# Pacing a weave by VectorE work and moving one block's queries and softmax one dense layer ahead, in a two-layer linear-attention kernel

## The chip, the cores and the metric

The kernel runs on one core of a Trainium2 chip. The metric is device time in microseconds (us) of one execution; the time before is the median of 3 runs. Engines are named as the profile names them: PE (TensorE, matrix multiplications and transposes), PEld (its weight loads), DVE (VectorE), ACT (ScalarE), POOL (GpSimd) and SP (SyncE, which here issues nearly all transfers). Each engine works through its own queue in order, so an instruction that waits holds up all that stand behind it on that engine.

## The reference

Two layers, each an attention block A and a dense block B, with the same weights in both layers. There are 2048 rows of D = 576, 32 heads of 18, and a hidden width F = 4608.

```
x = A_x
x = x + A(layernorm(x));  x = x + B(layernorm(x))      # layer 0
x = x + A(layernorm(x));  x = x + B(layernorm(x))      # layer 1

A(x): q, k, v = x @ wqkv, split into 32 heads of 18
      pq, pk = q @ w_phi, k @ w_phi                    # per head, 18x18
      phi(p) = concat(softmax(p), softmax(-p))         # 36 features
      kv = sum over rows of phi(pk)^T v;  z = sum over rows of phi(pk)
      o  = (phi(pq) @ kv) / (phi(pq) . z + 1e-6)
      return o @ wo
B(x): r = relu(x @ w1 + b1);  return (r*r) @ w2 + b2
```

## The kernel before

**Tiling.** The 2048 rows are four blocks of 512, each four tiles of 128 rows. A product in float32 accuracy is made of three products of rounded parts: each operand is split into a high part (an ACT copy to the type fp32r) and a low part (the operand less its high part, on DVE or POOL). Every such split therefore is an ACT instruction with a DVE or POOL instruction behind it. Names that end in `h` and `l` are these two parts.

**Dense layer** (`g_mlp`). For one block it walks over 36 slices f of the hidden width. A step loads the slice's weights (`m_0r` in the trace), splits them into `m_0h` (of w1) and `m_0s` (of w2), makes the hidden values `m_0ph` in 14 matmuls, squares and splits them into `m_0hb`, and adds the slice before to the output `m_0acc` in 15 matmuls. On DVE a step is three subtractions: `m_0h` (L696), `m_0s` (L697, a part of it on POOL at L698) and `m_0hb` (L718). Each step ends with a `yield`.

**Attention of a block** (`g_attend`), also a generator of small steps: `g_q` makes the four query tiles on PE (`a_3q`, `a_3qp`), `g_soft` the two softmaxes of a tile (DVE, POOL, ACT; tiles `Q0` to `Q3`), `g_phi` the normaliser (two steps a tile, tiles `m` and `u`), `g_out` transposes the features and multiplies them by kv (eleven steps, tiles `pt`, `fh`, `fl`, `pn`, `oh`, `ol`), and the norm steps multiply by wo (`po`), add the residual and normalise, so that the next dense layer can begin. `g_out` has two PSUM buffers in these stages: one holds `pt`, the other the open sum `pn`.

**The weave.** `weave(main, other, rate)` runs a dense layer and takes `rate` steps of the next blocks' attention per dense step, each step counting 1 whatever it holds. Behind the weave stands a scheduler that gives each engine its order: an instruction may be moved ahead of others on its engine where the scheduler thinks that the engine would stand idle. `tc.issue_after` limits this: what is written under it stays behind a named instruction of the same engine. `held` puts a generator's steps behind the latest `m_..hb`.

**Layer 1**, which is all that the change touches. The stages are, in order: a barrier that finishes the attention of block 1 (names `t1`); the dense layer of block 1 (`m_1`), woven with the attention of block 0 (`a_0`) at rate 1.0; the dense layer of block 0 (`m_0`), woven with the attention of blocks 3 and 2 (`a_3`, `a_2`) at rate 2.2; and last `g_pair`, the dense layer of blocks 3 and 2 taken together with seven products of half size in place of eight. `g_norm_first` and `g_norm_second` prepare the pair's operands: the second one forms sums and differences of the two blocks' halves in `combine` (names `a_2nu`, `a_2nt1` and so on, many small operations on DVE, POOL and ACT). The pair's own weights go through `load_pair` and `split_pair` (names `m_3r`, `m_3w`, `m_3s`). Before its loop the pair does this for its first two slices:

```
        drain(split_pair(0, load_pair(0)))
        raw = load_pair(1)
        for k in range(NP):
```

`split_pair(0)` borrows one of the two buffers `h1` and one of the two buffers `r1`, through which the dense layer before moves its own weights `m_0h` and `m_0r`.

Of the kernel before, what the change touches and what calls it, by code (L numbers as in the profile page):

```python
# [7 lines left out]
F32 = mybir.dt.float32  # L8
# [5 lines left out]
P = 128  # L14
TB = 512
# [6 lines left out]
def layers_kernel(  # L22
# [19 lines left out]
    S, D = x_in.shape[1], x_in.shape[2]  # L42
# [9 lines left out]
    NC = KC + 1  # L52
# [9 lines left out]
    TP = 3 * TW  # L62
# [32 lines left out]
    def drain(gen):  # L95
        for _ in gen:
            pass

    def weave(main, other, rate):

        due = 0.0
        for _ in main:
            due += rate
            while due >= 1.0 and next(other, other) is not other:
                due -= 1.0
        drain(other)

    def lagged(n, produce, consume, by=1):

# [63 lines left out]
    def new_slot(t, name, dtype=F32):  # L173
        return cst.tile([P, NC * P], dtype, name=name, tag=f"vslot{t}")
# [378 lines left out]
    def held(gen):  # L553

        while True:
            with tc.issue_after(dense["last"].ins):
                done = next(gen, gen) is gen
            if done:
                return
            yield  # L560

    def g_soft(raws, er, name, apart=0):
        for t in range(NT):
# [23 lines left out]
            ph.append(e)  # L587
            yield

    def g_out(layer, b, ph, dst, name, parts=1, pause=None, behind=None, norm=None):  # L590

# [51 lines left out]
        for part in range(parts):  # L643
            for _ in lagged(2 * NG, lambda i: turn(part, i), lambda i, f: times(part, i, f), parts):
                if pause and part < parts - 1:
                    next(pause, None)
                yield
        yield
        pair = pair or pieces()

        def x_after(t):
# [17 lines left out]
            nc.gpsimd.tensor_add(x, x, b2t)  # L669
            nc.sync.dma_start(xm[b][t], x)  # L670

        yield from (norm or g_norm)(x_after, dst, f"{name}n", keep)


    def g_mlp(layer, b, x, after, name, behind=None):
# [165 lines left out]
    def g_norm_second(x_of, dst, name, then):  # L841
# [4 lines left out]
            return t[:, : HK * TB].rearrange("p (c n) -> p c n", c=HK)  # L846

        def prepare():
            for a, k in enumerate(("b11", "b21")):
                cols = slice(a * HK * TB, (a + 1) * HK * TB)  # L850
                hi, lo = (sb.tile([P, 2 * D], F32, tag="E", name=f"{name}{k}{p}", bufs=4)[:, : HK * TB] for p in "hl")
                nc.sync.dma_start(hi, pth[:, cols])
                nc.sync.dma_start(lo, ptl[:, cols])
                full.append(new_slot(a, f"{name}f{a}")[:TP, :TB])
                nc.sync.dma_start(full[a], ptt[:, a * TB : (a + 1) * TB])
                ops[k] = [two(hi.bitcast(F32R)), two(lo.bitcast(F32R))]

# [57 lines left out]
    def g_pair(layer, blocks, x, after, name):  # L915

        R = D - P
        accs, wide, high, wops = {}, {}, {}, {}
        accs[0] = [ps_a.tile([P, TB], F32, tag=f"acc{c}", name=f"{name}acc{c}") for c in range(NC)]

        def load_pair(k):
            tags = ((cst, "zb"), (sb, "xd")) if k % 2 == 0 else ((cst, "kbh"), (cst, "kbl"))
            cols = slice(2 * k * P, 2 * (k + 1) * P)
            raw = []
            for a, (pool, tag) in enumerate(tags):
                r = pool.tile([P, (HK + 1) * 2 * P], F32, tag=tag, name=f"{name}r{a}_{k}", bufs=1)
# [139 lines left out]

        drain(split_pair(0, load_pair(0)))
        raw = load_pair(1)
        for k in range(NP):
            f0, f1 = 2 * k, 2 * k + 1  # L1070
            prep = split_pair(k + 1, raw) if k + 1 < NP else iter(())
# [55 lines left out]
            return x  # L1127
        return get

    def g_attend(layer, b, x, raws, dst, name, behind=None, norm=None):  # L1130

        if raws is None:
            raws = []
            if x is None:
                x = unspill(b, f"{name}u")
            yield from g_q(x, wpair("q", name), raws, name)
        er, ph = [], []
        yield from held(g_soft(raws, er, name))
        yield from held(g_phi(layer, er, ph, name, True))
        yield from g_out(layer, b, ph, dst, name, behind=behind and behind["last"], norm=norm)  # L1140

    def barrier(layer, b, prev, x, xprev, kes, vpair):

# [60 lines left out]
    for layer in range(2):  # L1204
        ready, raws = barrier(layer, b, prev, x, xprev, kes, vpair)
        spare["tags"] = []
        nxt_raws = raws
        prev_rows = None
        for i, b in enumerate(order):
            n = f"{layer}_{b}"  # L1210
            if layer and i == 2:
                drain(g_pair(layer, order[2:], operands, rows, f"m{n}"))
                break
            nxt = {}
            keep = {}
            operands = {}

            def g_back(i=i, prev_rows=prev_rows, keep=keep, nxt=nxt, nxt_raws=nxt_raws, operands=operands):
                if prev_rows is not None:
                    pb, rows = prev_rows  # L1220
                    m = f"1_{pb}"
                    xk = {}
                    yield from g_norm(lambda t: rows[t], xk, f"n{m}")
                    if i < NB - 1:
                        spill(pb, xk)
                        vts = []
                        yield from g_v(xk, wpair("v", f"w{m}"), vts, f"v{m}")
                        es = []
                        yield from g_k(xk, wpair("k", f"w{m}"), es, f"k{m}",
                                       then=lambda t: kv_tile(1, vts[t], es[t], f"kv{m}_{t}"))  # L1230
# [50 lines left out]
```

## Time and profile before

| | |
|---|---|
| median of 3 runs | 2591.77 us (2591.14 to 2592.89) |
| the profiled execution | 2591.81 us |
| its span, first to last instruction | 2590.1 us |
| mean granted clock of PE | 0.988 |
| busy share: PE, PEld, DVE, ACT, POOL | 97%, 85%, 59%, 49%, 31% |
| layer 1: start of `m_1`, of `m_0`, of the pair | about 1521, 1782 and 2137 us |

The page gives the busy share of each engine over the span and in 40 slices; asked for stretches, the trace gives each engine's busy time in them with the granted clock of PE, that is the share of its full speed at which PE was let run. A stretch loses time in two ways: PE stands idle, or it works at a lower clock. The list of waits says which instruction stood waiting and for what; the list in order of time gives each instruction's start and duration, with the idle time before it in square brackets.

### The profile page before, as it was taken

How to read it: one execution, taken by the hardware profiler on the slowest of the kernel's cores; microseconds unless marked ns; L12 is line 12 of the kernel's file. 1: busy time of each engine (PE TensorE's matmuls, PEld its weight loads, DVE VectorE, ACT ScalarE, POOL GpSimd, SP SyncE). 2: the span in 40 equal slices, each digit the busy share in tenths (PEclk: the TensorE clock that was granted, in tenths of full speed). 3: DMA queues.
4: the chain of work that ended last, by engine and by line, in shares of the span. 5: the costliest groups of instructions: out<-in, count | busy, mean ns of one | idle time of the engine just before them, and what ended most of it. 6: DMA issues, size and time to landing. Idle time of an engine off the chain costs nothing.

```text
span 2590.1 us, 41423 instructions
## 1 busy us (share of the span) xinstructions
PE 2519.7 (97%) x15282; PEld 2211.0 (85%) x15282; DVE 1533.6 (59%) x2408; ACT 1266.7 (49%) x2177; POOL 797.6 (31%) x869
## 2 busy tenths in 40 slices
PE   8999999999999999999999999999899988999999
PEld 8998888888888888888889988889788776888888
DVE  7778844446755458466334987344856656544444
ACT  4344554445554445545544445534445445666543
POOL 3444311113222123123111523121322257555222
PEclk9998999999999999999999999999999998999999
DMA  7103333354334443343332234235334324333364
GB/s 249 57 22 95 99 114 93 112 178 126 97 87 140 142 126 101 88 153 97 101 97 85 57 94 129 83 105 180 92 95 160 97 92 138 110 101 109 102 200 153
DMA packets 276758, 295.03 MB, mean 114 GB/s; under 512 B 28906, under 2 KB 206826, under 8 KB 274250
## 3 DMA queue, kind: packets, MB, share of 16 engines
q1 hardware_dynamic: 275296, 289.68, 37.1%
q8 instruction: 119, 1.95, 0.3%
q10 hardware_dynamic: 1258, 2.70, 0.3%
q14 instruction: 85, 0.70, 0.1%
HBM read 249.39 MB, written 42.89 MB: 113 GB/s over the span
## 4 chain that ended last, share of the span: by engine, by line
PE 50%; DVE 7%; POOL 2%; issue 1%; ACT 1%; DMA 0%; DVEq 0%; POOLq 0%; SPq 0%; ACTq 0%
PE m_1ph L708 8%; PE m_1acc L735 6%; PE m_0ph L708 5%; PE m_3px L988 4%; PE m_0acc L735 4%; PE m_3acc L1017 3%; PE m_3acacc L1017 2%; PE m_3py L988 2%; PE m_1acc L726 2%; PE m_0acc L726 1%; PE m_3acacc L1007 1%; PE m_3pz L988 1%; PE m_3acc L1007 1%; PE m_3ach L1017 1%; PE t1opo L662 1%
## 5 line engine op out<-in xcount | busy, mean ns | idle before, releaser
L708 PE MATMUL m_0ph<-a_0nh,m_0h 128*128 128x512 f32 (+1 forms) x760 | 199.7, 389 | 8.0 <-DVE m_0h L696 7.9
L735 PE MATMUL m_0acc<-m_0s,m_0hb 128*128 128x448 f32 x864 | 201.7, 368 | 1.5 <-DVE m_0hb L718 1.5
L735 PE MATMUL m_1acc<-m_1s,m_1hb 128*128 128x448 f32 x864 | 199.3, 366 | 1.4 <-DVE m_1hb L718 1.4
L735 PEld LDWEIGHTS m_0acc<-m_0s,m_0hb 128*128 128x128 f32 x864 | 162.8, 189 | 24.0 <-DVE m_0hb L718 2.8
L735 PEld LDWEIGHTS m_1acc<-m_1s,m_1hb 128*128 128x128 f32 x864 | 161.8, 188 | 23.1 <-DVE m_1hb L718 2.3
L698 POOL TENSOR_TENSOR m_0s<-m_0r,m_0s 128x128 fp32r<-128x128 f32 x72 | 58.0, 806 | 361.2 <-ACT m_0s L694 331.2
L708 PEld LDWEIGHTS m_0ph<-a_0nh,m_0h 128*128 128x128 f32 x760 | 137.9, 191 | 36.4 <-DVE m_0h L696 9.9
L698 POOL TENSOR_TENSOR m_1s<-m_1r,m_1s 128x128 fp32r<-128x128 f32 x72 | 59.3, 824 | 322.1 <-ACT m_1s L694 312.6
L696 DVE TENSOR_TENSOR m_1h<-m_1r,m_1h 128x640 fp32r<-128x640 f32 x72 | 64.9, 902 | 155.4 <-ACT m_1h L693 155.4
L696 DVE TENSOR_TENSOR m_0h<-m_0r,m_0h 128x640 fp32r<-128x640 f32 x72 | 66.6, 926 | 122.0 <-ACT m_0h L693 119.4
L715 ACT ACTIVATE m_0hr<-m_0ph,b1t 128x512 f32<-128x512 f32 x72 | 49.4, 686 | 180.5 <-PE m_0ph L708 180.5
L715 ACT ACTIVATE m_1hr<-m_1ph,b1t 128x512 f32<-128x512 f32 x72 | 49.5, 687 | 171.5 <-PE m_1ph L708 171.5
L977 DVE TENSOR_TENSOR m_3s<-m_3r,m_3s 128x448 fp32r<-128x448 f32 x72 | 49.5, 688 | 95.3 <-ACT m_3s L976 93.5
L735 PE MATMUL m_2acc<-m_2s,m_2hb 128*128 128x448 f32 x432 | 99.7, 366 | 1.3 <-DVE m_2hb L718 1.3
L735 PE MATMUL m_3acc<-m_3s,m_3hb 128*128 128x448 f32 x432 | 99.6, 366 | 0.9 <-DVE m_3hb L718 0.9
L978 POOL TENSOR_TENSOR m_3s<-m_3r,m_3s 128x128 fp32r<-128x128 f32 x72 | 58.0, 805 | 134.5 <-ACT m_3s L976 127.9
L708 PE MATMUL m_2ph<-a_2nh,m_2h 128*128 128x512 f32 (+1 forms) x380 | 97.3, 384 | 0.3 <-DVE m_2h L696 0.3
L708 PE MATMUL m_3ph<-t0onh,m_3h 128*128 128x512 f32 (+1 forms) x380 | 95.7, 382 | 0.1
L708 PE MATMUL m_1ph<-t1onh,m_1h 128*128 128x512 f32 (+1 forms) x380 | 95.7, 382 | 0.0
L708 PE MATMUL m_1ph<-a_1nh,m_1h 128*128 128x512 f32 (+1 forms) x380 | 95.3, 381 | 0.0
L1017 PE MATMUL m_3acc<-m_3s,m_3hb 128*128 128x448 f32 x432 | 94.4, 366 | 0.1
L735 PEld LDWEIGHTS m_2acc<-m_2s,m_2hb 128*128 128x128 f32 x432 | 80.8, 188 | 12.3 <-DVE m_2hb L718 2.2
(2103 smaller groups left out, 7096.9 us busy)
## 6 DMA issues: line engine op xcount, KB each, us to landing
m_3r<-in_B_w SPq DMA_DIRECT2D x108, 288.0 KB
m_0r<-in_B_w SPq DMA_DIRECT2D x72, 288.0 KB
m_1r<-in_B_w SPq DMA_DIRECT2D x72, 288.0 KB
m_3r<-in_B_w SPq DMA_DIRECT2D x72, 256.0 KB
m_0r<-in_B_w SPq DMA_DIRECT2D x72, 256.0 KB
m_1r<-in_B_w SPq DMA_DIRECT2D x72, 256.0 KB
m_2r<-in_B_w SPq DMA_DIRECT2D x36, 288.0 KB
m_2r<-in_B_w SPq DMA_DIRECT2D x36, 256.0 KB
```

What stands on the lines that cost most here:

```text
L662: nc.tensor.matmul(pt[:, :HP], a, m[:w, g], start=(g == 0 and k == 0), stop=(g == NG - 1 and k == 2))
L696: nc.vector.tensor_sub(l1, r1, h1.bitcast(F32))
L698: nc.gpsimd.tensor_sub(s2[:, D + R : 2 * D], r2[:, R:], s2[:, R:D].bitcast(F32))
L708: nc.tensor.matmul(ph[:, cols], a, m, start=(k == 0), stop=(k == len(ops) - 1))
L715: nc.scalar.activation(hr, ph, AF.Relu, bias=b1t[:, f : f + 1])
L726: nc.tensor.matmul(acc[KC], a, m, start=(f == 0 and k == 0), stop=(f == NF - 1 and k == 2))
L735: nc.tensor.matmul(acc[t][:, :R], a[:, rows], m, start=(f == 0 and k == 0), stop=(f == NF - 1 and k == 2))
L977: nc.vector.tensor_sub(s2[:, D : D + R], r2[:, :R], s2[:, :R].bitcast(F32))
L978: nc.gpsimd.tensor_sub(s2[:, D + R : 2 * D], r2[:, R:], s2[:, R:D].bitcast(F32))
L988: nc.tensor.matmul(ps, a, m, start=start and i == 0, stop=i == len(ms) - 1, skip_group_check=True)
L1007: nc.tensor.matmul(accs[b][KC], a, m, start=(g == 0 and k == 0), stop=(g == NF - 1 and k == 2))
L1017: nc.tensor.matmul(accs[b][t][:, :R], a[:, rows], m, start=(g == 0 and k == 0), stop=(g == NF - 1 and k == 2))
```

## The change

It changes four things in layer 1; layer 0 keeps its order.

1. A step of the woven generators now yields a cost, and `weave` subtracts that cost in place of 1. The costs are 5.5 for a softmax tile, 2.8 for a half step of `g_phi`, 1.0 for a step of `g_q` and `g_out`, and 3.0 for a step of the norm. The rate, now in the same unit, is 3.0 for `m_1` and 4.8 for `m_0`.
2. The queries of block 3 move into the weave with `m_1`, ahead of the `g_out` of block 0, and the softmax of block 3 moves to between the `g_out` and the norm of block 0. In the weave with `m_0` block 3 then begins with `g_phi`.
3. The pair's generator is made early; its first call (`split_pair(0)` and the loads of slice 1) comes at the end of the weave with `m_0` and no longer after it.
4. Buffers: the even slices of the pair now load into `kbh` and `kbl`, the odd ones into `zb` and `xd` (before it was the other way round), the small tile `full` of `g_norm_second` goes to `zb`, and the pair takes its PSUM sums only after its first call.

```
-            while due >= 1.0 and next(other, other) is not other:
-                due -= 1.0
+            while due >= 1.0:
+                cost = next(other, other)
+                if cost is other:
+                    break
+                due -= cost or 1.0
...
+    def paced(gen, cost):
+        for _ in gen:
+            yield cost
...
-                yield
-        yield
+                yield costs[0]
+        yield costs[0]
+        if mid:
+            yield from mid
         pair = pair or pieces()
...
-        yield from (norm or g_norm)(x_after, dst, f"{name}n", keep)
+        yield from paced((norm or g_norm)(x_after, dst, f"{name}n", keep), costs[1])
...
+            rests = cst.tile([P, 2 * D], F32, name=f"{name}f", tag="zb")
...
-                full.append(new_slot(a, f"{name}f{a}")[:TP, :TB])
+                full.append(rests[:TP, a * TB : (a + 1) * TB])
...
-        accs[0] = [ps_a.tile([P, TB], F32, tag=f"acc{c}", name=f"{name}acc{c}") for c in range(NC)]
...
-            tags = ((cst, "zb"), (sb, "xd")) if k % 2 == 0 else ((cst, "kbh"), (cst, "kbl"))
+            tags = ((cst, "kbh"), (cst, "kbl")) if k % 2 == 0 else ((cst, "zb"), (sb, "xd"))
...
         drain(split_pair(0, load_pair(0)))
         raw = load_pair(1)
+        yield
+        accs[0] = [ps_a.tile([P, TB], F32, tag=f"acc{c}", name=f"{name}acc{c}") for c in range(NC)]
...
-    def g_attend(layer, b, x, raws, dst, name, behind=None, norm=None):
...
+    def g_attend(layer, b, x, raws, dst, name, behind=None, norm=None, mid=(None, None), er=None):
+
+        cost = (lambda c: c) if layer else (lambda c: None)
+        if er is None:
+            er = []
+            if raws is None:
+                raws = []
+                yield from g_queries(layer, b, x, raws, name)
+            yield from paced(held(g_soft(raws, er, name)), cost(5.5))
+        ph = []
+        yield from paced(held(g_phi(layer, er, ph, name, True)), cost(2.8))
+        if mid[0]:
+            yield from mid[0]
+        yield from g_out(layer, b, ph, dst, name, behind=behind and behind["last"], norm=norm, mid=mid[1],
+                         costs=(cost(1.0), cost(3.0)))
+
+    def g_queries(layer, b, x, raws, name):
+        cost = (lambda c: c) if layer else (lambda c: None)
+        if x is None:
+            x = unspill(b, f"{name}u")
+        yield from paced(g_q(x, wpair("q", name), raws, name), cost(1.0))
...
+        pair = g_pair(layer, order[2:], operands, None, f"m{layer}_p")
...
             if layer and i == 2:
-                drain(g_pair(layer, order[2:], operands, rows, f"m{n}"))
+                drain(pair)
                 break
...
-                if layer and i == 1:
-                    for j, norm in ((2, g_norm_first), (3, g_norm_second)):
-                        yield from g_attend(layer, order[j], None, None, operands, f"a{layer}_{order[j]}", None, norm)
+                if layer and i == 0:
+                    m, later = f"a{layer}_{order[2]}", []
+                    mid = (g_queries(layer, order[2], None, later, m), paced(held(g_soft(later, early, m)), 5.5))
+                    yield from g_attend(layer, order[1], None, nxt_raws, nxt, f"a{layer}_{order[1]}", dense, None, mid)
+                elif layer:
+                    yield from g_attend(layer, order[2], None, None, operands, f"a{layer}_{order[2]}", None,
+                                        g_norm_first, er=early)
+                    yield from g_attend(layer, order[3], None, None, operands, f"a{layer}_{order[3]}", None, g_norm_second)
+                    next(pair)
...
-            weave(g_mlp(layer, b, ready, rows, f"m{n}", None if i else dense["turned"]), g_back(), 1.0 if i == 0 else 2.2 if layer else 1.5)
+            weave(g_mlp(layer, b, ready, rows, f"m{n}", None if i else dense["turned"]), g_back(), (3.0, 4.8)[i] if layer else 1.5 if i else 1.0)
```

The scheduler's order shows three places where the change moves instructions. The first is DVE at the start of `m_1`, where the barrier's last norm tile (`t1ox` is the row tile, `t1ons` and `t1onm` its moments, `t1onn` the normalised tile that PE transposes) is made. Before:

```order
L665 TENSOR_TENSOR t1ox_15525<-t1opo_15527,t1ox_15525 128x288
L309 BN_STATS t1ons_15561<-t1ox_15525 128x6
L665 TENSOR_TENSOR t1ox_15525<-t1opo_15544,t1ox_15525 128x288
L309 BN_STATS t1ons_15561<-t1ox_15525 128x6
L310 BN_AGGR t1onm_15562<-t1ons_15561 128x2
L324 TENSOR_SCALAR t1onn_15569<-t1ox_15525,t1onm_15562,t1ond_15563 128x512
```

The same place on DVE now:

```order
L674 TENSOR_TENSOR t1ox_15525<-t1opo_15527,t1ox_15525 128x288
L316 BN_STATS t1ons_15561<-t1ox_15525 128x6
L296 TENSOR_TENSOR a_3q0l<-a_3q0r,a_3q0h 128x1440
L674 TENSOR_TENSOR t1ox_15525<-t1opo_15544,t1ox_15525 128x288
L296 TENSOR_TENSOR a_3q1l<-a_3q1r,a_3q1h 128x1440
L316 BN_STATS t1ons_15561<-t1ox_15525 128x6
L348 TENSOR_TENSOR t1onl<-t1onp_15574,t1onh 128x4x128
L317 BN_AGGR t1onm_15562<-t1ons_15561 128x2
L331 TENSOR_SCALAR t1onn_15569<-t1ox_15525,t1onm_15562,t1ond_15563 128x512
```

The two splits of block 3's query weights (`a_3q0l`, `a_3q1l`) now stand inside that norm tile's chain.

The second place is DVE at the start of `m_0`, where the first attention work of block 3 follows on the dense step's `m_0h_3` and `m_0hb`. Before:

```order
L696 TENSOR_TENSOR m_0h_4_18259<-m_0r_4_18253,m_0h_4_18259 128x640
L718 TENSOR_TENSOR m_0hb_18213<-m_0hr_18212,m_0hb_18213 128x512
L415 TENSOR_REDUCE a_3Q0m<-a_3qs_18038 128x32
L416 TENSOR_REDUCE a_3Q0m<-a_3qs_18038 128x32
L697 TENSOR_TENSOR m_0s_3_18191<-m_0r_3_18185,m_0s_3_18191 128x448
L419 TENSOR_TENSOR a_3Q0e<-a_3qs_18038,a_3Q0m 128x576
L415 TENSOR_REDUCE a_3Q1m<-a_3qs_18071 128x32
```

The same place on DVE now:

```order
L705 TENSOR_TENSOR m_0h_3_18256<-m_0r_3_18250,m_0h_3_18256 128x640
L727 TENSOR_TENSOR m_0hb_18190<-m_0hr_18189,m_0hb_18190 128x512
L582 TENSOR_TENSOR a_3m_18211<-a_3Q0e,zb_14901 128x576
L583 TENSOR_REDUCE a_3u_18210<-a_3m_18214 128x32
L583 TENSOR_REDUCE a_3u_18210<-a_3m_18211 128x32
L582 TENSOR_TENSOR a_3m_18224<-a_3Q1e,zb_14901 128x576
```

The softmax of block 3 is gone from here, and its normaliser (`a_3m`, `a_3u`) comes at once.

The third place is DVE at the end of `m_0`. Before, the dense step's `m_0h_35` comes just ahead of the first `combine` of block 2 (`a_2nu`), and the pair's first weights follow much later:

```order
L696 TENSOR_TENSOR m_0h_35_20924<-m_0r_35_20918,m_0h_35_20924 128x640
L718 TENSOR_TENSOR m_0hb_20832<-m_0hr_20831,m_0hb_20832 128x512
L885 TENSOR_TENSOR a_2nu_20875<-a_2np_20852,a_2nb11h 128x256
L697 TENSOR_TENSOR m_0s_34_20810<-m_0r_34_20804,m_0s_34_20810 128x448
L887 TENSOR_TENSOR a_2nu_20875<-a_2nu_20875,a_2nb11l 128x256
```

The end of `m_0` on DVE now (the pair's weights are called `m_pw` here):

```order
L887 TENSOR_TENSOR a_2nt4t<-a_2nu_20944,a_2nt4t 32x256
L963 TENSOR_TENSOR m_pwv_0_20980<-m_ps_0_20972,m_pwv_0_20980 128x256
L887 TENSOR_TENSOR a_2nh<-a_2np_20938,a_2nh 32x256
L887 TENSOR_TENSOR a_2nt3t<-a_2nu_20944,a_2nt3t 32x256
L963 TENSOR_TENSOR m_pwv_0_20981<-m_ps_0_20973,m_pwv_0_20981 128x256
L963 TENSOR_TENSOR m_pwa_20976<-m_ps_0_20975,m_pwa_20976 128x256
L963 TENSOR_TENSOR m_pwa_20976<-m_ps_0_20974,m_pwa_20976 128x256
L705 TENSOR_TENSOR m_0h_34_21025<-m_0r_34_21019,m_0h_34_21025 128x640
L706 TENSOR_TENSOR m_0s_34_21026<-m_0r_34_21020,m_0s_34_21026 128x448
L727 TENSOR_TENSOR m_0hb_21048<-m_0hr_21047,m_0hb_21048 128x512
L727 TENSOR_TENSOR m_0hb_21097<-m_0hr_21096,m_0hb_21097 128x512
L705 TENSOR_TENSOR m_0h_35_21074<-m_0r_35_21068,m_0h_35_21074 128x640
```

All of block 2's `combine` and the pair's first weights now stand ahead of `m_0h_34`, and `m_0h_35` stands behind the second `m_0hb` after it.

More of the change, by code (lines that the diff above doesn't have):

```diff
@@ L556, in held @@
             with tc.issue_after(dense["last"].ins):
-                done = next(gen, gen) is gen
-            if done:
+                cost = next(gen, gen)
+            if cost is gen:
                 return
-            yield
+            yield cost
     def g_soft(raws, er, name, apart=0):
@@ L588, in g_phi, with g_out @@
             yield
-    def g_out(layer, b, ph, dst, name, parts=1, pause=None, behind=None, norm=None):
+    def g_out(layer, b, ph, dst, name, parts=1, pause=None, behind=None, norm=None, mid=None, costs=(None, None)):
         kbh, kbl = sums[layer]["kb"]
@@ L646, in g_out @@
                     next(pause, None)
-                yield
-        yield
+                yield costs[0]
+        yield costs[0]
+        if mid:
+            yield from mid
         pair = pair or pieces()
@@ L1128, in load_x @@
         return get
-    def g_attend(layer, b, x, raws, dst, name, behind=None, norm=None):
[L1132 to L1140, printed above, removed]
+    def g_attend(layer, b, x, raws, dst, name, behind=None, norm=None, mid=(None, None), er=None):
[17 more added lines that the diff above has]
+        yield from paced(g_q(x, wpair("q", name), raws, name), cost(1.0))
     def barrier(layer, b, prev, x, xprev, kes, vpair):
@@ L1208, in layers_kernel @@
         prev_rows = None
+        early = []
+        operands = {}
+        pair = g_pair(layer, order[2:], operands, None, f"m{layer}_p")
         for i, b in enumerate(order):
@@ L1215, in layers_kernel, with g_back @@
             keep = {}
-            operands = {}
-            def g_back(i=i, prev_rows=prev_rows, keep=keep, nxt=nxt, nxt_raws=nxt_raws, operands=operands):
+            def g_back(i=i, prev_rows=prev_rows, keep=keep, nxt=nxt, nxt_raws=nxt_raws):
                 if prev_rows is not None:
```

## The prediction

> **What bounds the kernel now.** The head of the page comes first, because it says how little there can be to gain.
>
> ```profile
> PE 2519.7 (97%) x15282; PEld 2211.0 (85%) x15282; DVE 1533.6 (59%) x2408; ACT 1266.7 (49%) x2177; POOL 797.6 (31%) x869
> ```
>
> PE is the bound. The change adds no product and removes none, so it can only win back time in which PE stands or works at a lower clock, or lose more of it. The second view, the busy time in stretches of 20 us, finds these places in layer 1. The columns are stretch, length, then PE, PEld, DVE, ACT and POOL busy (instructions), granted clock, DMA share and GB/s.
>
> ```profile
> 1520.00:1540.00 20.00, 19.06 (x121) 17.39 (x120) 12.64 (x22) 11.84 (x21) 6.22 (x7) 1.00 0.33 104
> 1540.00:1560.00 20.00, 19.06 (x87) 15.77 (x86) 20.00 (x26) 13.00 (x20) 6.37 (x6) 1.00 0.39 109
> 1820.00:1840.00 20.00, 17.28 (x74) 14.40 (x73) 19.06 (x24) 12.81 (x19) 8.71 (x7) 0.91 0.17 47
> 1840.00:1860.00 20.00, 16.10 (x63) 12.28 (x62) 19.45 (x34) 6.77 (x11) 10.06 (x8) 0.91 0.21 63
> 2000.00:2020.00 20.00, 18.68 (x85) 15.62 (x84) 19.88 (x33) 10.15 (x17) 9.50 (x8) 1.00 0.28 79
> 2020.00:2040.00 20.00, 14.98 (x62) 11.93 (x61) 13.29 (x20) 6.05 (x11) 5.67 (x5) 0.83 0.35 98
> 2100.00:2120.00 20.00, 16.73 (x89) 14.42 (x88) 10.98 (x25) 8.89 (x19) 13.11 (x17) 1.00 0.13 45
> 2120.00:2140.00 20.00, 13.25 (x58) 9.35 (x56) 16.60 (x40) 11.77 (x30) 14.31 (x21) 0.94 0.31 91
> 2140.00:2160.00 20.00, 13.66 (x42) 9.14 (x42) 13.11 (x23) 8.07 (x16) 14.67 (x19) 0.72 0.46 148
> ```
>
> I count as loss the idle time of PE plus its busy time times (1 - clock). Rows 1 and 2 lose 0.94 each. Rows 3 and 4 lose 2.72 + 3.90 idle and 0.09 x (17.28 + 16.10) = 3.0 of clock: 9.6 us (place B). Rows 5 and 6 lose 1.32 + 5.02 and 0.17 x 14.98 = 2.5: 8.9 us (place C). The last three lose 3.27 + 6.75 + 6.34 = 16.4 idle and 0.06 x 13.25 + 0.28 x 13.66 = 4.6 of clock: 21.0 us (place D). All of it is 41 us, so nothing I can name would bring the kernel much below 2551 us.
>
> The list of PE's waits in these stretches names the causes (us in total, times, longest).
>
> ```profile
> PE m_0ph L708 <- DVE m_0h L696: 6.1, 3, 2.7
> PE a_2pt L615 <- DVE a_2Q3e L585: 5.0, 1, 5.0
> PE a_2np L805 <- DVE a_2nl L904: 3.3, 1, 3.3
> PE m_0py L771 <- DVE a_2nl L904: 2.7, 1, 2.7
> PE m_3px L988 <- DVE m_3wv L954: 2.5, 1, 2.5
> PE m_3py L988 <- ACT m_3wv L953: 1.9, 1, 1.9
> PE t1onp L339 <- DVE t1onn L324: 0.9, 1, 0.9
> ```
>
> The first row is B: the dense layer's weight split stands on DVE behind softmax and normaliser work. The second is C: the first transpose of block 2 waits for the last normalised tile. The next four are D: the combinations of block 2, then the pair's first weights. The last is the barrier before `m_1` (place A).
>
> **B and C: the softmax spread out.** A dense step needs this on DVE (min/median/max in ns):
>
> ```profile
> L696 DVE TENSOR_TENSOR m_0h<-m_0r,m_0h x34: 755/825/1792, 1790.8 to 2105.9; 128x640 fp32r<-128x640 f32 x34
> L697 DVE TENSOR_TENSOR m_0s<-m_0r,m_0s x36: 555/624/1831, 1787.6 to 2120.1; 128x448 fp32r<-128x448 f32 x36
> L718 DVE TENSOR_TENSOR m_0hb<-m_0hr,m_0hb x36: 675/692/1917, 1792.4 to 2128.1; 128x512 fp32r<-128x512 f32 x36
> ```
>
> That is 0.825 + 0.624 + 0.692 = 2.1 us. On PE its 29 matmuls take 29 x 19.06/87 = 6.35 us by the second stretch, so DVE has 4.2 us a step for attention. A softmax tile costs it this (in order of time):
>
> ```profile
> 1816.28 0.74 DVE L416 TENSOR_REDUCE a_3Q0m<-a_3qs 128x32 f32<-128x576 f32 x1
> ...
> 1817.48 1.73 DVE L419 TENSOR_TENSOR a_3Q0e<-a_3qs,a_3Q0m 128x576 f32<-128x576 f32 x1
> ...
> 1820.50 1.35 DVE L423 TENSOR_REDUCE a_3Q0r<-a_3Q0e 128x64 f32<-128x1152 f32 x1
> 1821.77 0.75 DVE L419 TENSOR_TENSOR a_3Q1e<-a_3qs,a_3Q1m 128x576 f32<-128x576 f32 x1
> 1822.43 0.55 DVE L424 RECIPROCAL a_3Q0r<-a_3Q0r 128x64 f32<-128x64 f32 x1
> ```
>
> Two reductions of 0.74 (L415 is of the same size as L416), a subtraction of 0.75 to 1.73, 1.35 and 0.55 make 4.1 to 5.1, say 4.6 us. For the normaliser I take what is left: DVE is busy 38.5 us in rows 3 and 4; their 137 matmuls are at most 4.7 dense steps (10.1 us); the other 28.4 us are about three softmax tiles (14) and four normaliser tiles (14), so 1.8 us for half a tile. At 2.2 steps of any kind a dense step was given up to 2.2 x 4.6 + 2.1 = 12.2 us of DVE work against 6.35 on PE. That is B and C.
>
> After the change the softmax of block 3 runs in `m_1` at 3.0/5.5 = 0.55 tile a step: 2.5 + 2.1 = 4.6 us, covered. The normaliser in `m_0` gives 4.8/2.8 x 1.8 + 2.1 = 5.2 us, and the softmax of block 2 4.8/5.5 x 4.6 + 2.1 = 6.1, to 6.6 with long subtractions. These fit, barely. I leave 1 us of loss at each place (bounds 0 and 2.5): **B gains 8.6, C gains 7.9.** At C the transpose also no longer follows four tiles at once: the normaliser's halves come one or two a step.
>
> A rule that speaks against this: the Trainium skill, "SBUF — State Buffer", section "Who interferes with whom", says that a DVE instruction with two SBUF inputs contends with a GpSimd instruction that reads SBUF, and that the second to issue blocks fully. The trace agrees in that L419 takes 0.75 us and 1.73 us on equal tiles, though no row shows the cause. If every such subtraction were a long one, a softmax step would come to 6.6 us and C would gain 6.4.
>
> **A: the start of `m_1`.** The query weights of block 3 are now split where the barrier ends. Below are the row of one such split in the trace of before, and in order of time the norm that PE waits for at the barrier and PE's products behind it:
>
> ```profile
> L289 DVE TENSOR_TENSOR a_3q0l<-a_3q0r,a_3q0h x1: 1658/1658/1658, 1777.4 to 1777.4; 128x1440 fp32r<-128x1440 f32 x1
> 1523.10 0.55 DVE L324 TENSOR_SCALAR t1onn<-t1ox,t1onm,t1ond 128x512 f32<-128x512 f32 x1 [0.99 <-POOL t1ond L312]
> 1525.67 1.35 PE L708 MATMUL m_1ph<-t1onh,m_1h 128*128 128x256 f32 x10
> ```
>
> Two of these subtractions, 2 x 1.66 = 3.3 us, stand on DVE ahead of `t1onn`, where DVE is free for at most the 0.99 us in brackets. Queued behind are `t1onn` and `t1onl`, for which PE waits. PE has in the new order 16 more half-wide products ahead of that transpose (1.35/10 = 0.13 us each, 2.2 us), so its wait grows from 0.9 to about 2.7, and some 0.6 us of splits behind the transposes lose their cover: 2.4 us of idle time. At B 3.0 us of clock went with 6.6 of idle, 0.45 for each us; here that is 1 to 1.5. The 0.94 of row 2, where DVE was full, goes (3.0 counts a step now instead of one of any size, and a softmax tile is 5.5). **A loses 3.0** (bounds 0, if PE finds more to do, and 8, if the queries, whose operand is loaded at that same time, are late too and hold `m_1ph` behind them).
>
> On the clock the trace shows 0.91 in rows 3 and 4 although no wait on `m_0h` there is over 2.7 us. The Trainium skill, "TensorE: Matmul & The Clock Gate", section "Part 1: The HAM clock gate", lets the clock fall only after an idle window of about 3.4 us; by it A would cost no clock and the time would be 1.5 us less. The rows differ from it, and I go by them.
>
> **Denser `g_out`.** A turn of `g_out` (transpose on PE, copy on ACT, rest on DVE) takes one buffer for its whole length:
>
> ```profile
> 1894.31 0.27 PE L615 MATMUL a_3pt<-ident,a_3Q0e 128*72 128x128 f32 x1
> ...
> 1895.57 0.69 DVE L618 TENSOR_TENSOR a_3fl<-a_3pt,a_3fh 72x512 fp32r<-72x512 f32 x1 [1.58 <-ACT a_3fh L617]
> ```
>
> From 1894.31 to 1896.26 that is 1.95 us. PE's own part of a turn, four transposes and three products of 512 columns, I estimate at 1.14 us from the matmul rate above. There were two turns a dense step in `m_0`; now a turn costs 1.0 of 4.8, so four or five fall together. Spread among 29 matmuls they fit (4.8 x 1.95 = 9.4 us against 6.35 + 4.8 x 1.14 = 11.8). Clumped, each leaves up to 0.8 us. With 30 turns (three blocks of ten) I take 0.1 us each: **loses 3.0** (bounds 0 and 8).
>
> **D: the end of `m_0`.** The attention now ends about 3 steps before the dense layer does (its costs are 4 x 5.5 for softmax, 16 x 2.8 for the normaliser and 90 in steps of 1 and 3, together 156.8; at 4.8 a dense step that is 32.7 of 36), and the pair's first weights follow at once. Before, POOL's first sums of the pair came late (the group's row: instructions, busy time and mean, then the idle time ahead of them):
>
> ```profile
> L961 POOL TENSOR_TENSOR m_3s<-m_3r,m_3r 128x384 f32<-128x384 f32 x7 | 7.5, 1076 | 10.6 <-DMA m_3r<-in_B_w 10.2
> ```
>
> And these are the first and the last instruction of one combination on DVE:
>
> ```profile
> 2108.10 0.42 DVE L885 TENSOR_TENSOR a_2nu<-a_2np,a_2nb11h 128x256 f32<-128x256 f32 x1 [0.34 <-PE a_2np L805]
> ...
> 2117.96 0.42 DVE L904 TENSOR_TENSOR a_2nl<-a_2np,a_2nh 128x256 fp32r<-128x256 f32 x1 [2.80 <-ACT a_2nh L903]
> ```
>
> The 10.2 us of waiting for the load goes (other buffers, free earlier), and with it 2.5 + 1.9 of PE's waits and the clock of 0.72. But two combinations, each 10.3 us long on DVE by the two rows (2108.10 to 2118.38), stand ahead of `m_0hb` of steps with 6 to 7 us of PE work: 2.6 and 4.2 us late, as I work it out. `m_0h` of step 34 stands on DVE behind splits of the pair's weights, which wait for four sums on POOL (4 x 1.08) behind POOL's share of the combinations: about 3.4. The last steps have one `h1` and one `r1` buffer, since the pair holds the others: 1.5; clock 0.5. Of 21.0 that leaves 12.2: **D gains 9** (bounds -3, if the last steps also wait for each other's loads, and 18). The loads of the pair are issued on SP ahead of those of the last dense steps, which is in the 1.5.
>
> **Sum.** 8.6 + 7.9 + 9 - 3 - 3 = 19.5 us. The profiled execution took 2591.8 us (span 2590.1 and 1.7 around it), which is the median; so 2591.8 - 19.5 = **2572.3 us**.
>
> **The rivals.**
> - *All of it comes back.* B 9.6, C 8.9, D 18, A 1: 37.5, **2554 us**. For it: PE may be fed by the reordering that the scheduler does. Against: the combinations are as long on DVE as before, and now meet a denser weave.
> - *The pair's first weights starve the last steps of `m_0`*, and D only moves some 20 us earlier: D gains 0, **2581 us**. For it: the single buffers, and the splits that wait for POOL on DVE. Against: PE still has the combinations' transposes to do.
> - *Slower: `g_out` runs at the speed of its round trip.* If the turns stand next to each other on PE, each leaves 0.8 us: 30 x 0.8 = 24, with clock 1.45 x 24 = 35, against gains of 22.5 without `g_out`: **2604 us**. It decides from 22.5/30 = 0.75 us a turn, clock included. Against it: in the new order dense matmuls stand between most turns.
> - *The stalls only move.* DVE does the same work, and if its long tiles stall PE once wherever they are put, nothing changes: **2590 us**. Against it: the second stretch shows DVE full for 20 us with 0.94 us of PE lost.
>
> **How the numbers follow.** Forecast 0.62, full gain 0.14, starved end 0.12, slow `g_out` 0.07, moved stalls 0.05. A measurement of this kernel can tell about 0.2% from no change, 5.2 us: the limits are 2586.6 and 2597. The forecast with A, `g_out` and D at their poor ends together (0.01 each for same and slower) adds to the last two: faster 0.86, same 0.06, slower 0.08. The range runs from the full gain, 2554, to 2586, which takes in the starved end with A at 8; outside lie the last two rivals and a little of the forecast.
>
> **What would show it.** Right: in the waits of after, `m_0ph <- m_0h` is gone near the start of `m_0` and `a_2pt <- a_2Q3e` is gone; `t1onp <- t1onn` has grown to about 2.7; the pair's first products wait neither for `m_3wv` nor for its like; and new waits of `m_0acc` on `m_0hb` and of `m_0ph` on `m_0h` stand in the last six steps of `m_0`, about 10 us together. Wrong: PE rows below 19 us of 20 in the stretches of the `g_out`s (the slower rival), a loss of 9 us or more around the softmax in `m_1` or `m_0` (moved stalls), or 20 us lost at the end of `m_0` (starved end).

## The result and the profile after

The changed kernel takes 2573.74 us in the median of 4 runs (2570.49 to 2576.19), beside 2592.33 us before: 18.6 us less, a ratio of 0.9928 with a 95% interval of 0.9911 to 0.9945. In a second comparison it took 2572.91 beside 2593.01 (0.9923, 0.9909 to 0.9937). The forecast was 2572.3. The profiled execution of after is the fastest of the first four, 2570.49 us with a span of 2568.8, 21.3 less than the span before.

The head of the page and the stretches of after follow, with the same columns as in the prediction; two stretches are added, 2080 to 2100 and 2160 to 2180, since the tail of `m_0` begins earlier now.

```profile
PE 2508.2 (98%) x15282; PEld 2205.1 (86%) x15282; DVE 1536.7 (60%) x2408; ACT 1266.5 (49%) x2177; POOL 801.5 (31%) x869
1520.00:1540.00 20.00, 17.19 (x109) 15.46 (x109) 13.16 (x19) 8.98 (x14) 4.54 (x6) 1.00 0.83 261
1540.00:1560.00 20.00, 20.00 (x93) 17.15 (x92) 16.84 (x22) 13.44 (x22) 5.62 (x5) 1.00 0.39 114
1820.00:1840.00 20.00, 18.04 (x87) 14.91 (x85) 19.89 (x29) 10.30 (x17) 9.37 (x8) 1.00 0.38 115
1840.00:1860.00 20.00, 20.00 (x104) 16.00 (x105) 10.80 (x17) 11.30 (x20) 0.90 (x1) 1.00 0.21 59
2000.00:2020.00 20.00, 17.49 (x90) 14.25 (x89) 14.81 (x24) 10.18 (x18) 3.51 (x4) 1.00 0.35 102
2020.00:2040.00 20.00, 20.00 (x109) 16.49 (x109) 11.74 (x21) 8.72 (x16) 2.53 (x4) 1.00 0.51 166
2080.00:2100.00 20.00, 16.96 (x74) 13.46 (x73) 14.30 (x30) 11.18 (x27) 12.38 (x18) 0.91 0.23 66
2100.00:2120.00 20.00, 13.97 (x53) 11.19 (x52) 12.43 (x20) 10.31 (x20) 11.10 (x13) 0.83 0.49 146
2120.00:2140.00 20.00, 17.90 (x82) 14.45 (x80) 15.79 (x27) 12.23 (x25) 14.89 (x20) 1.00 0.50 162
2140.00:2160.00 20.00, 18.36 (x81) 15.21 (x82) 9.93 (x17) 13.41 (x25) 13.01 (x18) 1.00 0.42 127
2160.00:2180.00 20.00, 20.00 (x92) 16.89 (x91) 10.99 (x18) 13.72 (x26) 13.54 (x18) 1.00 0.41 118
```

Counted as in the prediction (idle time and busy time at a lower clock), place A loses 2.8 us now (1.9 before), B 2.0 (9.6), C 2.5 (8.9). For D the whole of 2080 to 2200 us is compared: 16.7 now (4.6 + 8.4 + 2.1 + 1.6), 23.0 before, with 2.0 behind 2160 us. Together 24.0 against 43.4, so 19.4 of the 21.3 us by which the spans differ; the rest is within what these rows round away and two executions differ by. The list of PE's waits over layer 1 up to 2220 us says what is left.

```profile
PE m_0ph L717 <- ACT m_0hr L724: 6.6, 3, 6.0
PE m_0acc L744 <- DVE m_0hb L727: 2.4, 3, 1.6
PE t1onp L346 <- DVE t1onn L331: 2.2, 1, 2.2
PE a_2np L814 <- DVE a_2nh L887: 2.2, 1, 2.2
PE m_ppx L997 <- DVE m_pz L1091: 1.9, 1, 1.9
PE m_ppx L997 <- DVE m_pu L1104: 1.8, 1, 1.8
PE m_0ph L717 <- DVE m_0h L705: 1.4, 1, 1.4
PE a_2pn L638 <- DVE a_2fl L625: 0.9, 1, 0.9
PE a_3pn L638 <- DVE a_3fl L625: 0.6, 1, 0.6
```

The 5.0 us of `a_2pt` are gone, and of the 7.4 us of `m_0ph` on `m_0h` that the same list of before has, 1.4 are left. The pair's first products wait for no weights; where they wait it is for the steps that work on their own earlier sums (`m_pz`, `m_pu`). The first row is new, and is the largest wait of the layer: 6.0 us at the end of `m_0`, in the stretch with the 8.4 us of loss. The list puts it down to `m_0hr`; ACT's own order of time shows what held `m_0hr` up:

```profile
2102.95 0.52 ACT L962 ACTIVATE m_pwv<-m_ps 128x384 fp32r<-128x384 f32 x1 [0.54 <-POOL m_ps L972]
...
2104.70 0.52 ACT L962 ACTIVATE m_pwa<-m_ps 128x384 fp32r<-128x384 f32 x1 [0.65 <-POOL m_ps L975]
2105.84 0.52 ACT L962 ACTIVATE m_pwa<-m_ps 128x384 fp32r<-128x384 f32 x1 [0.61 <-POOL m_ps L977]
2106.27 0.72 ACT L702 ACTIVATE m_0h<-m_0r 128x640 fp32r<-128x640 f32 x1
2106.89 0.67 ACT L724 ACTIVATE m_0hr<-m_0ph,b1t 128x512 f32<-128x512 f32 x1
```

The copies of the pair's first weights wait one after another for POOL's sums `m_ps`, and the dense layer's `m_0h` and `m_0hr` stand behind them in ACT's queue.

### The profile page after: what moved, and what is told of

It reads as the page before. It is cut to its first block, busy times and chain, and to the rows that moved or that the text cites. A ratio compares the mean times of both kernels' runs of the same rounds, so it can differ in the third digit from the quotient of the medians.

```text
span 2568.8 us, 41380 instructions
## 1 busy us (share of the span) xinstructions
PE 2508.2 (98%) x15282; PEld 2205.1 (86%) x15282; DVE 1536.7 (60%) x2408; ACT 1266.5 (49%) x2177; POOL 801.5 (31%) x869
## 4 chain that ended last, share of the span: by engine, by line
PE 52%; DVE 6%; POOL 1%; issue 1%; ACT 1%; DMA 0%; DVEq 0%; ACTq 0%; POOLq 0%; SPq 0%
PE m_1ph L717 9%; PE m_1acc L744 7%; PE m_0ph L717 5%; PE m_ppx L997 5%; PE m_pacc L1026 3%; PE m_0acc L744 3%; PE m_pacacc L1026 3%; PE m_ppy L997 2%; PE m_1acc L735 2%; PE m_ppz L997 1%; PE m_pacacc L1016 1%; PE m_pacc L1016 1%; PE m_0acc L735 1%; PE m_pach L1026 1%; PE a_0po L671 1%
## 5 line engine op out<-in xcount | busy, mean ns | idle before, releaser
L986 DVE TENSOR_TENSOR m_ps<-m_pr,m_ps 128x448 fp32r<-128x448 f32 x72 | 51.2, 711 | 95.8 <-ACT m_ps L985 94.9
L987 POOL TENSOR_TENSOR m_ps<-m_pr,m_ps 128x128 fp32r<-128x128 f32 x72 | 59.0, 819 | 136.2 <-ACT m_ps L985 128.1
L744 PE MATMUL m_3acc<-m_3s,m_3hb 128*128 128x448 f32 x432 | 99.6, 366 | 1.0 <-DVE m_3hb L727 1.0
L1026 PE MATMUL m_pacc<-m_ps,m_phb 128*128 128x448 f32 x432 | 94.1, 366 | 0.0
L985 ACT ACTIVATE m_ps<-m_pr 128x576 fp32r<-128x576 f32 x72 | 49.1, 683 | 88.6 <-PE m_pacacc L1016 63.7
```

The source lines that it names most:

```text
L744: nc.tensor.matmul(acc[t][:, :R], a[:, rows], m, start=(f == 0 and k == 0), stop=(f == NF - 1 and k == 2))
L985: nc.scalar.activation(s2[:, :D], r2, AF.Copy)
L986: nc.vector.tensor_sub(s2[:, D : D + R], r2[:, :R], s2[:, :R].bitcast(F32))
L987: nc.gpsimd.tensor_sub(s2[:, D + R : 2 * D], r2[:, R:], s2[:, R:D].bitcast(F32))
L1026: nc.tensor.matmul(accs[b][t][:, :R], a[:, rows], m, start=(g == 0 and k == 0), stop=(g == NF - 1 and k == 2))
```

## The experiments

Each is compared with runs of the kernel before on the same chip. The first question was how the gain splits between the parts, above all what the early call of the pair is worth, which in the traces seemed to win 11 us in one stage and lose 8 in another.

**The pair's call after the weave** (`e1_pair_late`):

```
-                    next(pair)        # in the weave with m_0
```

> As changed, but the pair's first call comes after the weave again. Theory P (the early call wins 11.0 us in the pair's stage but brings about 8.4 us of loss with it, because the pair's ACT copies wait for POOL's sums ahead of the last steps' copies of m_0): about 2576 us, with a pair's stage about 11 us longer, the 6.0 us wait of m_0ph gone and the stretch before the pair about 8 shorter. Rival F (the losses before the pair belong to the combinations of block 2, and the early call is clear gain): about 2585. Rival N (the early call is worth nothing): 2574.

Measured: 2570.79 us beside 2592.76 (0.9914, 0.9901 to 0.9928), 22.0 less. That is 2 to 3 us below the changed kernel, a gain that no theory had, though the intervals of the two ratios overlap. The 6.0 us wait is gone, and the loss from 2080 to 2200 us is 11.0 us in place of 16.7. The pair still starts on time (2125.9 us, 2126.5 in after), and its stage takes 445.0 us, 2.7 more than in after. ACT's order of time shows how: the scheduler itself draws the pair's copies ahead, but now they stand between those of `m_0`.

```profile
2106.17 0.51 ACT L962 ACTIVATE m_pwb<-m_pr 128x384 fp32r<-128x384 f32 x1
...
2110.36 0.73 ACT L702 ACTIVATE m_0h<-m_0r 128x640 fp32r<-128x640 f32 x1
2110.99 0.62 ACT L726 ACTIVATE m_0hr<-m_0hr 128x512 f32<-128x512 f32 x1
2112.00 0.53 ACT L962 ACTIVATE m_pwv<-m_ps 128x384 fp32r<-128x384 f32 x1 [0.40 <-POOL m_ps L970]
```

**The early call alone** (`e2_pair_only`), on the kernel before, with the new buffers:

```
+                    next(pair)        # at the end of the weave, rate 2.2 as before
-            tags = ((cst, "zb"), (sb, "xd")) if k % 2 == 0 else ((cst, "kbh"), (cst, "kbl"))
+            tags = ((cst, "kbh"), (cst, "kbl")) if k % 2 == 0 else ((cst, "zb"), (sb, "xd"))
```

> The kernel before with the early call of the pair and its buffers alone: no costs, nothing moved. Theory P: about 2589 us (11 us won in the pair's stage, about 8 lost before it), with the losses at 1820 to 1860 and 2000 to 2040 us as before (9.6 and 8.9). Rival F: about 2581. Rival N: 2592.

Measured: 2591.36 beside 2592.76 (0.9994, 0.9985 to 1.0002): no change that can be told. The pair starts 4 us earlier and takes 4 us longer. Its first products no longer wait for weights, but now for `m_pz` (`m_ppy`, 4.3 us). Theory P had expected 3 us less here, and that the late call in the run before would cost about 2 us; both came out otherwise, so the 11 us had another source.

**The count of one** (`e3_flat_count`), with the move and the early call kept:

```
-                due -= cost or 1.0
+                due -= 1.0
-  (3.0, 4.8)[i] if layer
+  (1.15, 2.12)[i] if layer
```

> As changed, but each step counts 1 again (rates 1.15 for m_1 and 2.12 for m_0, so that both weaves end at the same dense step). Theory C (the count is what spreads softmax): softmax of block 2 costs DVE 2.12 x 4.6 + 2.1 = 11.9 us a step against 6.35 on PE, so about 6 us come back at 2000 to 2040 us and 1 to 3 at the softmax in m_1: about 2581 us. Rival M (the move alone carries the gain, and the count is worth nothing): 2574.

Measured: 2581.91 beside 2592.76 (0.9959, 0.9945 to 0.9972), 10.9 less than before and 8 to 9 more than as changed. Theory C foresaw the size, but not the places: against the changed kernel the loss grows most at B, from 2.0 to 5.9 us, then in 2080 to 2180 us, from 16.7 to 19.3, and least at C, from 2.7 to 3.9 (counted from 1980 us here). At B it is the normaliser of block 3 and no softmax that PE waits for (`a_3pt` on `a_3Q3e`, 3.1 us).

**Sums first** (`e5_sums_first`):

```
             if k == 0:
+                (POOL's four sums)
+                yield                 # one dense step
+                (copies of a11, a12, s1, s2)
+                yield                 # one dense step
+                (copies of s4, s3, a22)
```

> As changed, but the pair's first call is cut in three steps, one dense step apart: POOL's four sums first, then the copies of four operands, then of three. Theory P: ACT no longer stands behind sums that POOL hasn't made, the 6.0 us wait of m_0ph goes with about 2 us of clock: about 2567 us (2565 to 2570). Rival: POOL is late with the sums wherever the copies stand, or the last steps then wait for DVE instead: 2573 to 2575.

Measured: 2569.73 beside 2592.76 (0.9909, 0.9895 to 0.9922), 23.0 less. The wait is down to 2.0 us, and the loss from 2080 to 2200 us to 11.4. The queue on ACT was indeed what cost; but the call after the weave does as well without any of this.

**What shortens the pair's stage.** Theory E took the place of P: the stage is shorter because block 2's attention ends three steps earlier, so that DVE and POOL are free for the pair's weights. Its rival B was the buffers. Two runs part them. `e6_old_buffers` leaves parts 1 and 2 alone:

```
-            tags = ((cst, "kbh"), (cst, "kbl")) if k % 2 == 0 else ((cst, "zb"), (sb, "xd"))
+            tags = ((cst, "zb"), (sb, "xd")) if k % 2 == 0 else ((cst, "kbh"), (cst, "kbl"))
-                    next(pair)
```

> Parts 1 and 2 alone: costs and move, the pair's call after the weave and its buffers as before (even slices in zb and xd). Theory E (the pair's stage got shorter because the attention ends three steps earlier, which leaves DVE and POOL free for the pair's splits): 2571 us, as with the late call. Rival B (it got shorter because slice 0 now loads into kbh and kbl, free since block 2's g_out; in zb and xd its load waits for the end of m_0): POOL waits for the load again, some 10 us, and about 8 of them on PE: 2579.

Measured: 2570.73 beside 2593.01 (0.9914, 0.99 to 0.9928), 22.3 less, as E has it. `e10_only_rate` is the kernel before with one number changed:

```
-  1.0 if i == 0 else 2.2 if layer else 1.5
+  1.0 if i == 0 else 2.4 if layer else 1.5
```

> The kernel before with one number changed: the rate of the weave in m_0 is 2.4 in place of 2.2, so that the attention ends in step 32 or 33 of 36 and no longer in step 35. No costs, no move, no early call, old buffers. Theory E (the pair's stage got shorter because the attention ends earlier): the pair's stage is 8 to 11 us shorter and the combinations now lose PE's time inside m_0, 0 to 3 us net; at the softmax places the loss grows by some 2: 2583 to 2586 us. Rival (the end of the attention doesn't matter by itself, costs or move are needed): 2591 to 2594.

Measured: 2583.46 beside 2593.71 (0.9962, 0.9949 to 0.9976): 10.3 us, about half of the whole gain, from one digit. The attention does end earlier: the last transposes of block 2 (`a_2np`) start 13.2 us ahead of the last `m_0ph`, where before they stood 9.0 us behind it. The list of PE's waits up to 2220 us has no pair's weights in it any more. Its first two rows follow, and below them the first row of the same list of before:

```profile
PE m_0ph L708 <- DVE m_0h L696: 11.8, 4, 4.7
PE a_2np L805 <- DVE a_2nl L904: 4.7, 1, 4.7
```

```profile
PE m_0ph L708 <- DVE m_0h L696: 7.4, 4, 2.7
```

The waits for `m_0h` have grown by 4.4 us, but the 5.0 us of `a_2pt` on `a_2Q3e` are gone from the list. By the stretches B (1820 to 1880 us) loses 10.8 us in place of 9.7, and C 6.6 in place of 8.9, so together the softmax places are no worse; the 2 us of further loss that the expectation had there did not come.

The first products of the pair (first and last start in us) in before, e2, e10, after and e6:

```profile
L988 PE MATMUL m_3px<-a_2nb11h,m_3wv x36: 389/389/797, 2136.8 to 2434.1; 128*128 128x512 f32 x36
L988 PE MATMUL m_ppx<-a_2nb11h,m_pwv x36: 387/389/477, 2132.6 to 2433.9; 128*128 128x512 f32 x36
L988 PE MATMUL m_3px<-a_2nb11h,m_3wv x36: 389/389/494, 2137.7 to 2425.7; 128*128 128x512 f32 x36
L997 PE MATMUL m_ppx<-a_2nb11h,m_pwv x36: 389/389/396, 2126.5 to 2412.7; 128*128 128x512 f32 x36
L996 PE MATMUL m_ppx<-a_2nb11h,m_pwv x36: 389/389/498, 2122.0 to 2410.1; 128*128 128x512 f32 x36
```

From the first start to the end of the span the pair's stage takes 453.3 us before (2590.1 - 2136.8), 457.4 in e2, 444.0 in e10, 442.3 in after and 444.8 in e6. It is short wherever the attention ends early, with or without the early call and the new buffers. POOL's wait for the pair's loads, which was 10.2 us before, is about half of that in e10 and in e6, both with the old buffers (in after, with the new ones, it is 7.6):

```profile
L961 POOL TENSOR_TENSOR m_3s<-m_3r,m_3r 128x384 f32<-128x384 f32 x7 | 7.4, 1053 | 5.5 <-DMA m_3r<-in_B_w 5.1
L969 POOL TENSOR_TENSOR m_ps<-m_pr,m_pr 128x384 f32<-128x384 f32 x7 | 7.3, 1048 | 5.8 <-DMA m_pr<-in_B_w 5.4
```

The traces also show how the earlier end reaches the pair. With the old buffers one half of the pair's first load goes into `xd`, where the combinations keep `a_2ne`; SP starts it right behind their last transposes, and POOL's first sum needs it. The load and the sum in before, then in e10:

```profile
2131.30 0.38 SPq L928 DMA_DIRECT2D m_3r<-in_B_w  x1
2144.39 1.00 POOL L961 TENSOR_TENSOR m_3s<-m_3r,m_3r 128x384 f32<-128x384 f32 x1 [5.74 <-DMA m_3r<-in_B_w]
```

```profile
2117.16 0.38 SPq L928 DMA_DIRECT2D m_3r<-in_B_w  x1
2127.86 1.03 POOL L961 TENSOR_TENSOR m_3s<-m_3r,m_3r 128x384 f32<-128x384 f32 x1 [1.39 <-DMA m_3r<-in_B_w]
```

Before, the sum came 7.6 us behind the pair's first product; in e10 it comes 9.8 us ahead of it. A free buffer alone does not do it: in e2 this half loads into `kbl`, from 2082 us on, and still the sum comes at 2136.6, 3.9 us behind the first product, because the combinations stand ahead of it on POOL.

**Costs without the move** (`e7_no_move`): block 3's queries and softmax stay in `m_0`, the call stays late, rates 2.2 and 5.6.

```
-  mid = (g_queries(...), paced(held(g_soft(...)), 5.5))
-  (3.0, 4.8)[i] if layer
+  (2.2, 5.6)[i] if layer
```

> Part 1 with the new buffers, and the pair's call after the weave: block 3's queries and softmax stay in m_0. The rates are set so that both weaves end about where they do as changed: 2.2 for m_1, 5.6 for m_0. Theory S (the step of m_0 has 4.2 us of DVE to give; at 5.6 a softmax step needs 5.6/5.5 x 4.6 + 2.1 = 6.8 us, a normaliser step 5.7, so eight softmax tiles lose about 0.5 us each and the denser tail some 3 more): 2577 to 2580 us. Rival M (the move is most of the gain at the start of m_0): 2583 or more.

Measured: 2575.13 beside 2593.01 (0.993, 0.9917 to 0.9942), 17.9 less: better than S foresaw, and far from M. B's loss (1820 to 1880 us) falls to 3.8 us with no softmax moved at all, where e6 has about 2; C stays at 9.2, where e6 has 2.5. So most of what the move is worth lies at C and not at the place that it empties. The likely reason is that less work in `m_0` lets the rate be 4.8 instead of 5.6, so that block 2's softmax fits; no run here changes the rate without the move, so this is argued and not shown.

**The queries held back** (`e4_queries_held`), on the changed kernel:

```
-  mid = (g_queries(layer, order[2], None, later, m),
+  mid = (held(g_queries(layer, order[2], None, later, m)),
```

> As changed, but each step of block 3's queries stands behind the newest m_1hb on its engines, so that its weight splits can't stand in the barrier's norm. Theory A (the two splits hold up t1onn): the wait of t1onp falls from 2.2 to about 0.9 us and that of m_1ph on t1onh (0.6) goes: about 2572, 2 less than as changed. Rival: the queries then come too late for the softmax of block 3 or the barrier stands for something else: as changed or a little slower, 2574 to 2576.

Measured: 2570.56, beside 2593.01 before (0.9916, 0.9903 to 0.9929) and 2572.91 for the changed kernel once more:

> The changed kernel once more, beside the three that follow: 2573 to 2575 us for every theory.

So 2.4 us less, with ratios whose intervals overlap; the single runs, 2570.34 to 2571.86 against 2572.0 to 2573.6 us, do not. The loss at A falls from 2.8 to 0.9 us. The two lists show it, on DVE in after and among PE's waits in e4:

```profile
1520.12 1.67 DVE L296 TENSOR_TENSOR a_3q0l<-a_3q0r,a_3q0h 128x1440 fp32r<-128x1440 f32 x1
...
1522.08 1.64 DVE L296 TENSOR_TENSOR a_3q1l<-a_3q1r,a_3q1h 128x1440 fp32r<-128x1440 f32 x1
...
1525.80 0.55 DVE L331 TENSOR_SCALAR t1onn<-t1ox,t1onm,t1ond 128x512 f32<-128x512 f32 x1 [1.00 <-POOL t1ond L319]
```

```profile
PE t1onp L346 <- DVE t1onn L331: 0.9, 1, 0.9
```

**Both mends together** (`e8_best`): parts 1 and 2 as in e6, with the queries held.

> Parts 1 and 2 with the queries of block 3 held behind the newest m_1hb, the pair's call and buffers as before. Theory: the gains of the held queries (2.4 us beside the changed kernel) and of the late call (2.2) add up, since one lies at the start of m_1 and the other at the end of m_0: 2568 to 2569 us. Rival: they don't add, 2571.

Measured: 2568.08 beside 2593.71 (0.9903, 0.989 to 0.9917), 25.6 less; 5.5 us better than the changed kernel by the differences (25.6 and 20.1), though the intervals of the two ratios overlap a little. Adding the two mends to the 20.1 would give 24.7, so within 1 us they add; but by its interval e8 can't be told from e4 or e6, each with one mend. **A thinner tail** (`e9_thin_tail`) on top of that:

```
-  costs=(cost(1.0), cost(3.0))
+  costs=(cost(1.0), cost(4.0 if norm is g_norm_second else 3.0))
-  (3.0, 4.8)[i] if layer
+  (3.0, 5.0)[i] if layer
```

> The same with a cost of 4 in place of 3 for the norm steps of block 2 and a rate of 5.0 in place of 4.8, so that the combinations spread over more dense steps and end about two steps later. Theory L (the 4.4 us lost around 2080 to 2100 are combinations too dense on DVE, and the free steps at the end are more than the pair needs): 2565 to 2567 us. Rival E (the free steps are what shortened the pair's stage): the loss moves there, 2570 to 2573.

Measured: 2567.5 beside 2593.71 (the same ratio and interval): it can't be told from e8 by the time. The tail loses 1.1 us less at 2080 to 2100, and with the higher rate 3.1 us more are lost at 1820 to 1840. Rival E was not put to the test: the combinations begin earlier (2063.5 us, 2068.9 in e8) and do not end later, with their last transposes 20 us ahead of the last `m_0ph` in e9 and 19 in e8, and the pair's stage takes 444.0 and 444.7 us.

## Why the prediction was right, point by point

The time came out within 1.5 us of the forecast, and that is in good part luck: counted by the losses of the stretches, B, C and D gave 20.3 us where 25.5 were foreseen, and A and `g_out`, for which 6.0 of loss were set, took 0.9 (the waits of `g_out` lie within B and C and are counted there). The two errors, of 5.2 and 5.1 us, offset each other. The ladder of the runs, each against before in its own comparison: the attention's end moved three steps forward 10.3 (e10); the costs on top 7.6 (e7 less e10); the move on top 4.4 (e6 less e7); the early call and its buffers -2.2 (changed kernel less e6, whose ratios have overlapping intervals; the single runs are 2572.0 to 2573.6 and 2568.56 to 2571.98 us). Together 20.1, by the second comparison of the changed kernel. The first two steps stand clear of each other by their intervals; those of e7 and e6 overlap. The rungs are not pure either, since e7 and e6 also differ in their rates and buffers.

- **B and C** were foreseen with their mechanism, too much DVE work put into one dense step: 8.6 and 7.9, measured 7.7 and 6.4 by the losses of the stretches. Of what is left there, 0.6 and 0.9 us are the waits of `g_out`, which the sum held apart. That the count matters was shown by e3. That the move is what empties B was too strong a reading: in e7 the costs alone bring B to 3.8, and most of the move's gain shows at C.
- **`g_out`**: 3.0 us of loss foreseen, 1.5 seen (`a_3pn` 0.6 and `a_2pn` 0.9). The slower rival, a round trip in each of 30 turns, did not occur: the turns run at 1652 to 1682, 1837 to 1862 and 2006 to 2033 us, PE is busy for 20.00 of 20 us in the rows from 1840 and from 2020 us and loses nothing from 1640 to 1700, and the list has no wait for block 0's turns.
- **A**: the place, the two splits in the barrier's norm and the wait were right (2.2 us, foreseen 2.7). The 2.7 does not follow from the terms given with it: 0.9 + 3.3 - 2.2 is 2.0, and less if DVE's 0.99 us were free, which they were not (1.00 us still stands in brackets before `t1onn`). The size of the loss was not right: a net loss of 0.9 in the stretches and 2.4 by e4, for 3.0. What was too high is the clock. The rows read 1.00 in after for a term of 1 to 1.5 us. By the Trainium skill, "TensorE: Matmul & The Clock Gate", "Part 1: The HAM clock gate", the clock falls after an idle window of about 3.4 us, by which this wait would cost none: here after agrees, and of the five other executions with the same wait two don't (below).
- **D is where the working failed.** The step "the 10.2 us of waiting for the load goes (other buffers, free earlier), and with it 2.5 + 1.9 of PE's waits" put the gain down to the early call and the buffers. In e10 PE's waits on `m_3wv` are gone with neither of them, since the combinations end earlier; in e2, with both of them, others took their place and nothing was gained. Nor did POOL's wait for the loads go: 7.6 us of it are left in after. The size, 9, measured 6.3. The terms that were taken off it also went otherwise. Two late `m_0hb`, 6.8 us together, were foreseen, and PE's list has 0.5 us of that behind 2080 us; of the waits on `m_0h` foreseen for the last six steps it has none. The delay "on DVE behind splits of the pair's weights", 3.4 us, was 6.0 us and stood on ACT: I had followed the subtraction and not the copy ahead of it. The clock, put at 0.5, cost 3.9 in the two rows from 2080 to 2120 us (0.09 x 16.96 + 0.17 x 13.97). The rival of the starved end had the price of the early call about right, no gain, and a part of its mechanism, splits that wait for POOL; whether the single buffers cost anything no run tests. It took the rest of D to be zero too, which it was not.
- **All of it comes back** (2554 us) isn't reached even by the best versions, at 2568.

## What to carry to other kernels

Woven work that feeds the next stage should end some steps before the stage it is woven into; try the one number that sets its rate before any rearrangement, and look which buffer the next stage's first load waits for. If a step's cost differs by a factor of five, count it in time of the engine that it fills, and check that the quota of one main step fits. Work that is called early by hand goes into the queues at that place: if it waits for a slower engine, everything behind it on its own engine waits too, so look at the copy ahead of the subtraction, and ask if a scheduler already draws the work ahead where there is room.

## What was not expected of the hardware

The same wait need not cost the same clock. PE stood for 2.2 us before `t1onp` in after and in e1; the stretch has 17.19 us of busy PE in both, with a granted clock of 1.00 in the row of after shown above and of 0.91 here, in e1:

```profile
1520.00:1540.00 20.00, 17.19 (x117) 16.39 (x116) 11.88 (x22) 9.19 (x15) 4.45 (x7) 0.91 0.79 254
```

e5 shows 0.91 as well; the repeated after, e3 and e6 show 1.00. A clock term per stall, as I took it from B, is therefore a mean over executions at best.
